# A recorded kernel with its own list scheduler, and the second MLP started from one finished chunk

## The chip, the cores and the metric

The kernel runs on one core of a Trainium2 chip. The metric is the device time of one execution in microseconds; three runs of the kernel before gave 1299.58 to 1303.39 us, with a median of 1301.85 us. The engines are named as in the profile: PE (TensorE; PEld its weight loads), DVE (VectorE), ACT (ScalarE), POOL (GpSimd) and SP (SyncE, which issues all DMAs here).

## The reference

Top-k attention over 4 batches, 8 heads, 576 positions of 64, followed by two MLPs on 2304 tokens of width 512 with an inner width of 2048. All is float32.

```python
def _attn_ref(q, k, v):
    top_k = 32
    scores = scale * np.matmul(q, k.transpose(0, 1, 3, 2))
    kth = np.partition(scores, -top_k, axis=-1)[..., -top_k:-top_k + 1]
    scores = np.where(scores >= kth, scores, -1000000000.0)
    scores = scores - np.max(scores, axis=-1, keepdims=True)
    attn = np.exp(scores)
    attn = attn / (np.sum(attn, axis=-1, keepdims=True) + 1e-09)
    return np.matmul(attn, v)

x = attn_out.transpose(0, 2, 1, 3).reshape(B * S, H * D)
h = x @ w_in1;  x = softplus(h) @ w_out1
h = x @ w_in2;  x = (h - np.tanh(h)) @ w_out2
```

## The kernel before

**Precision.** Every float32 operand of a matmul is split into two float16 halves, `hi` and `lo`, and a product is three matmuls (hi hi, hi lo, lo hi). So the weights of both MLPs must first be converted: 4 matrices of 8 groups each (`whi0` to `whi3`, `wlo0` to `wlo3`). `weight_load` brings one group of 1 MB, `weight_convert` and `weight_split` work on it with four ACT passes, two DVE passes and three POOL passes; `conv_step` does the one for a new group and the other for the one before it. Groups that find no free place in memory are staged in four pieces of 256 columns.

**Attention.** There are 144 tiles of 128 query rows by 576 keys. For a tile, `front` makes the scores (`s`, PE; copied to `ssb` by ACT), `chain` finds the 32 largest with four MAX8 and three MATCH_REPLACE8 on DVE, each of which needs the one before it, and `exps` makes the exponentials on ACT. Where the exponential table is loaded, that takes two ACT passes; where the softplus table is loaded, `exps` uses softplus, and `mask` adds a masking pass on DVE (L600) and a scaling pass on ACT (L601). `turn` splits the result (`hl`, ACT and POOL), transposes it by DMA (`pT`), and `back` multiplies it with the values (`px`, PE: 14 matmuls of 65 columns, or 28 of a rest tile) and writes the tokens (`xs`, then `x` by a transposing DMA).

**MLPs.** The tokens form 8 chunks of 256 and 2 rest chunks of 128; they become complete after attention tiles 16, 36, 52, 72 (two), 88, 108, 128 (two) and 144. For each chunk and MLP there are 8 steps, one for each pair of weight groups. A step is `gemm1` (`h`, 24 matmuls), `act1` (softplus or tanh on ACT, then ACT, POOL and, in the second MLP, one DVE pass) and `gemm2` (`y`, 24 matmuls of 256 columns or 12 of 512). The first MLP needs the softplus table, the second the exponential table; `set_table` changes it.

**What sets the order.** The program is written tile by tile in a loop over `n`. In each turn stand the attention pieces of up to four tiles, then `emit_steps` (one step of 256 tokens a turn, as long as `next_step` finds one), then `conv_step` by a credit: two groups a turn until 16 are done, then, from turn 8, half a group a turn. `next_step` allows the second MLP when all 32 groups are done and at least `MINC` = 2 chunks have begun; it prefers the second MLP when `AHEAD` = 2 chunks wait for it, then a new chunk's first MLP, then the second MLP of a waiting chunk. On each engine the framework's scheduler, which simulates the program, then orders the instructions; `tc.high_priority(n)` moves a block ahead by n places: 50 for attention, 1000 for the matmuls of `back`, 100 for the first 16 weight groups. The order on each engine is then fixed, and each engine takes its instructions one after the other. PSUM has two banks for `s`, four shared by `h`, `px` and the small column sums `pn`, and two for `y`.

Of the kernel before, what the change touches and what calls it, by code (L numbers as in the profile page):

```python
# [38 lines left out]
MINC = 2  # L39
# [6 lines left out]
W2N = 8  # L46
# [23 lines left out]
HP = 50  # L70
HPB = 1000
# [3 lines left out]
def topk_attention_two_mlps(  # L75
# [17 lines left out]
    nc = tc.nc  # L93
# [14 lines left out]
    cp = ctx.enter_context(tc.tile_pool(name="cp", bufs=1))  # L108
    dp = ctx.enter_context(tc.tile_pool(name="dp", bufs=1, space=bass.MemoryType.DRAM))
    wp = ctx.enter_context(tc.tile_pool(name="wp", bufs=1))  # L110
    ap = ctx.enter_context(tc.tile_pool(name="ap", bufs=1))
    sp = ctx.enter_context(tc.tile_pool(name="sp", bufs=2))
    mp = ctx.enter_context(tc.tile_pool(name="mp", bufs=1))
    ps_s = ctx.enter_context(tc.tile_pool(name="ps_s", bufs=1, space=bass.MemoryType.PSUM))
    ps_t = ctx.enter_context(tc.tile_pool(name="ps_t", bufs=4, space=bass.MemoryType.PSUM))
    ps_y = ctx.enter_context(tc.tile_pool(name="ps_y", bufs=1, space=bass.MemoryType.PSUM))

    first = tc.keep_in_program_order(nc.scalar.preload_act_table_set(EXP_SET))  # L120
    table = [first, [], EXP_SET]

    def set_table(name):
        if table[2] == name:
            return
        with ExitStack() as es_:
            for i in table[1] or [table[0]]:
                es_.enter_context(tc.issue_after(i.ins))
            table[0] = nc.scalar.preload_act_table_set(name)
        table[1], table[2] = [], name  # L130

    def with_table(out, in_, func, **kw):

        with tc.issue_after(table[0].ins):
            table[1].append(nc.scalar.activation(out, in_, func, **kw))  # L135

    zq = cp.tile([P, 2, 2, 2, D], F16, name="zq")
# [3 lines left out]
    tiles_ = cp.tile([P, 224], F32, name="tiny")  # L143
# [22 lines left out]
    def col_norm(cols, n):  # L166

        ps = ps_t.tile([P, 512], F32, tag="tp", name=nm("pn"))
        for i in range(n):
            nc.tensor.matmul(ps[:, 0:1], ones.to_broadcast([P, P]), cols[:, i : i + 1],  # L170
                             start=(i == 0), stop=(i == n - 1))
        return ps[:, 0:1]

    def pow2_scale(ps, s, inv):

        n = sp.tile([P, 1], I32, tag="n0", name=nm("n0"))
# [948 lines left out]
```

## Time and profile before

| | |
|---|---|
| median of three runs | 1301.85 us |
| span of the profiled execution (its time from first to last instruction) | 1304.4 us |
| PE busy | 1007.8 us (77%) |
| DVE busy | 1020.7 us (78%) |
| ACT busy | 959.4 us (74%) |
| POOL busy | 844.0 us (65%) |

The page gives the profiled execution by its span; it is 2.5 us above the median. The busy shares are means over stages that differ: attention begins at once, the first MLP at some 230 us, and in the last 186 us there is nothing but MLP work. So the time has to be read by stage. A row of the view by stage reads: from and to, length, then busy us and the number of instructions of PE, PEld, DVE, ACT and POOL, the mean granted TensorE clock (1.00 is 2.4 GHz), the DMA engines' share and GB/s. A matmul's row in a timeline shows its latency; as matmuls are pipelined, its cost is the time to the next start.

### The profile page before, as it was taken

The numbers are of one execution on the slowest core, as the hardware profiler recorded it, in microseconds if no ns is written. First come the engines' busy times: TensorE is split into PE (matmuls) and PEld (weight loads), VectorE is DVE, ScalarE is ACT, GpSimd is POOL, SyncE is SP. The second block draws the span as 40 slices with busy tenths as digits, with TensorE's granted clock in tenths as the row PEclk, the third lists the DMA queues.
The fourth block names the chain that finished last, engine by engine and source line by source line (L and its number), as shares of the span: only waits on it lengthen the run. The fifth ranks groups of instructions, "written<-read, shape, count | busy, mean of one in ns | idle before, by whom it ended". The sixth has DMA issues, their size and how long they took to land.

```text
span 1304.4 us, 27426 instructions
## 1 busy us (share of the span) xinstructions
PE 1007.8 (77%) x9682; PEld 793.1 (61%) x9682; DVE 1020.7 (78%) x2183; ACT 959.4 (74%) x1924; POOL 844.0 (65%) x1194
## 2 busy tenths in 40 slices
PE   1221324884436999899799899998999899999998
PEld 1111213763325877668667787786768767986975
DVE  5897889999999998899698879988989799510020
ACT  7987989878878878876787678877777677733332
POOL 2789767787687667566587657667776476643332
PEclk9999999896557999999799989998999899999999
DMA  9955887456666757745456444444545344200000
GB/s 276 281 162 146 240 233 170 122 119 138 140 145 159 169 102 146 147 86 125 84 128 137 75 89 90 105 101 89 127 104 119 60 85 97 51 6 13 5 9 17
DMA packets 322522, 153.14 MB, mean 117 GB/s; under 512 B 270160, under 2 KB 302416, under 8 KB 322384
## 3 DMA queue, kind: packets, MB, share of 16 engines
q1 hardware_dynamic: 322384, 151.39, 51.1%
q8 instruction: 76, 1.25, 0.4%
q14 instruction: 62, 0.51, 0.1%
HBM read 73.04 MB, written 15.37 MB: 68 GB/s over the span
## 4 chain that ended last, share of the span: by engine, by line
PE 29%; DVE 22%; ACT 13%; DMA 13%; POOL 12%; issue 8%; SPq 2%; POOLq 0%; ACTq 0%; DVEq 0%
DVE m L576 7%; DVE x L579 7%; PE h L692 4%; PE h L691 4%; PE h L693 4%; DMA pT<-hl 2%; POOL hl L607 2%; PE y L735 2%; DMA qT<-qhl 2%; PE y L736 2%; PE y L734 2%; PE y L742 2%; PE y L743 2%; PE y L744 2%; POOL wlo L317 2%
## 5 line engine op out<-in xcount | busy, mean ns | idle before, releaser
L576 DVE MAX8 m<-x 128x8 f32<-128x576 f32 x432 | 320.2, 750 | 3.9
L607 POOL TENSOR_TENSOR hl<-x,hl 128x512 f16<-128x512 f32 x144 | 170.1, 1182 | 87.5 <-ACT hl L606 84.5
L713 POOL TENSOR_SCALAR r<-r,gs 128x512 f32<-128x512 f32 (+1 forms) x160 | 112.5, 704 | 160.9 <-ACT g L712 158.8
L579 DVE MATCH_REPLACE8 x<-m,x 128x576 f32<-128x576 f32 x288 | 213.4, 741 | 0.0
L564 PE MATMUL s<-kT,qT 128*128 128x288 f16 x512 | 120.2, 326 | 98.2 <-ACT ssb L567 69.9
L716 POOL TENSOR_TENSOR g<-r,g 128x512 f16<-128x512 f32 (+1 forms) x160 | 171.7, 1074 | 8.6
L734 PE MATMUL y<-g,whi 128*128 128x256 f16 (+1 forms) x640 | 163.1, 266 | 10.5 <-DVE y L763 6.9
L691 PE MATMUL h<-x,whi 128*128 128x256 f16 (+1 forms) x640 | 168.2, 271 | 3.6 <-ACT x L647 1.6
L692 PE MATMUL h<-x,whi 128*128 128x256 f16 (+1 forms) x640 | 168.0, 270 | 0.0
L693 PE MATMUL h<-x,wlo 128*128 128x256 f16 (+1 forms) x640 | 167.7, 270 | 0.0
L735 PE MATMUL y<-g,whi 128*128 128x256 f16 (+1 forms) x640 | 164.5, 267 | 1.4 <-POOL g L716 1.4
L691 PE MATMUL h<-y,whi 128*128 128x256 f16 (+1 forms) x640 | 164.6, 265 | 0.1
L736 PE MATMUL y<-g,wlo 128*128 128x256 f16 (+1 forms) x640 | 164.3, 267 | 0.0
L692 PE MATMUL h<-y,whi 128*128 128x256 f16 (+1 forms) x640 | 164.2, 265 | 0.0
L693 PE MATMUL h<-y,wlo 128*128 128x256 f16 (+1 forms) x640 | 163.9, 264 | 0.0
L710 DVE SCALAR_TENSOR_TENSOR r<-h,hin,r 128x512 f32<-128x512 f32 (+1 forms) x80 | 54.9, 689 | 134.0 <-ACT r L135 133.5
L135 ACT ACTIVATE r<-h,hin 128x512 f32<-128x512 f32 (+1 forms) x160 | 102.1, 640 | 70.0 <-PE h L693 56.8
L712 ACT ACTIVATE g<-r,gs 128x512 f16<-128x512 f32 (+1 forms) x160 | 107.6, 675 | 52.7 <-DVE r L710 21.0
L692 PEld LDWEIGHTS <-whi 128*128 128x128 f16 x1280 | 128.3, 100 | 23.4 <-issue 7.6
L691 PEld LDWEIGHTS <-whi 128*128 128x128 f16 x1280 | 128.4, 100 | 20.6 <-DMA x<-xs 0.6
L693 PEld LDWEIGHTS <-wlo 128*128 128x128 f16 x1280 | 128.6, 101 | 13.7
L135 ACT ACTIVATE x<-ssb,nb,tiny 128x576 f32<-128x576 f32 x144 | 123.7, 865 | 15.3 <-DVE m L576 10.8
(141 smaller groups left out, 3058.9 us busy)
## 6 DMA issues: line engine op xcount, KB each, us to landing
whi<-in_moe_w_in_dram SPq DMA_DIRECT2D x8, 1024.0 KB, 5.9
wlo<-in_moe_w_in_dram SPq DMA_DIRECT2D x6, 1024.0 KB, 6.8
wlo<-in_moe_w_out_dram SPq DMA_DIRECT2D x6, 1024.0 KB, 5.0
vd<-vhl SPq DMA_DIRECT2D x16, 330.0 KB, 3.0
vhl<-vd SPq DMA_DIRECT2D x16, 330.0 KB, 3.4
kd<-kT SPq DMA_DIRECT2D x32, 160.0 KB, 2.1
whi<-in_moe_w_out_dram SPq DMA_DIRECT2D x5, 1024.0 KB, 5.0
kT<-kd SPq DMA_DIRECT2D x32, 160.0 KB, 2.6
```

Of the source, the lines that this page charges most:

```text
L135: table[1].append(nc.scalar.activation(out, in_, func, **kw))
L564: nc.tensor.matmul(ps[:, hf, 0:HS], lhs, rhs[:, hf * HS : (hf + 1) * HS], start=(i == 0), stop=(i == len(prods) - 1))
L576: return lambda: nc.vector.max(m[:, 8 * i : 8 * i + 8], src)
L579: return lambda: nc.vector.match_replace(x, m[:, 8 * i : 8 * i + 8], src, NEG)
L607: nc.gpsimd.tensor_sub(hl[:, S + SL : 2 * S], st.p[:, 0 : NB * P], hl[:, 0 : NB * P])
L691: nc.tensor.matmul(o, hi[:, f], xhi, start=(d == 0), stop=False)
L692: nc.tensor.matmul(o, hi[:, f], xlo, start=False, stop=False)
L693: nc.tensor.matmul(o, lo[:, f], xhi, start=False, stop=(d == ND - 1))
L716: nc.gpsimd.tensor_sub(glo, r, ghi)
L734: nc.tensor.matmul(o, hi[:, dd], gh, start=first, stop=False)
L735: nc.tensor.matmul(o, hi[:, dd], gl, start=False, stop=False)
L736: nc.tensor.matmul(o, lo[:, dd], gh, start=False, stop=fin)
```

## The change

It has four parts.

1. All calls go through a `Recorder`. It keeps each instruction with its reads and writes (so that the order of conflicting ones stays), a price by engine and size, and a rank: its place in the program, less what `ahead(n)` takes off. `order` then plays the program: at each point the engine that can start earliest takes, of the instructions whose inputs are there, the one of lowest rank; PE prefers those that have been ready for `MARG` = 500 ns. A `burst` of matmuls (a `px`, an `s`, half a `gemm1` or `gemm2`) stays together.
2. Weight groups 16 to 31 are converted at one a tile from turn 0 on (in effect from turn 8, since the first 16 come at two a tile until then), instead of half a one from turn 8.
3. The second MLP may begin when one chunk has begun its first (`MINC` = 1).
4. Attention has `ahead(200)`, the first 16 weight groups 100 as before. PSUM's four shared banks become two for `h` and two for `px` and `pn`. Tiles are laid out by hand (`al`), round robin over the same numbers of buffers.

```diff
-MINC = 2
+MINC = 1
-W2N = 8
+W2N = 0
-HP = 50
-HPB = 1000
+HP = 200
+HPB = 50
+NH = 2
+NPX = 2
+MARG = 500.0
...
+class Recorder:
...
+    def ahead(self, n):
+        was = self.off
+        self.off = max(n, was)
+        yield
+        self.off = was
...
+    def price(self, eng, method, a, k, outs, ins):
+        n = max(math.prod(x.shape[1:]) for x in outs + ins)
+        if eng == "PE":
+            cols = math.prod(out.shape[1:])
+            return (max(31.0, cols / 2.4 + 2.5) if ins[0].dtype == F16 else 250.0), 350.0
+        if eng == "SP":
+            if "transpose" in method:
+                return 1350.0, 2000.0
+            size = math.prod(out.shape) * mybir.dt.size(out.dtype)
+            return 480.0, 2000.0 + size / 300.0
+        if eng == "ACT":
+            if method == "copy":
+                return 70 + 0.82 * n, 160.0
+            c = 90 + 0.88 * n
+            c += 50 * sum(isinstance(k.get(x), View) for x in ("bias", "scale"))
+            return c + (95 if k.get("accum_out") is not None else 0), 160.0
+        if eng == "DVE":
+            if method == "max":
+                return 670.0, 140.0
+            if method == "match_replace":
+                return 735.0, 140.0
+            if n <= 8:
+                return 75.0, 140.0
+            return 60 + 1.22 * n, 140.0
+        if method == "memset":
+            return 100 + 0.4 * n, 100.0
+        if method == "tensor_scalar":
+            return 280 + 0.97 * n, 100.0
+        return 150 + 1.95 * n, 100.0
...
+            while coming[e] and coming[e][0][0] <= t:
+                r, i = heapq.heappop(coming[e])
+                heapq.heappush(avail[e], (ops[i].rank, i))
+            i = None
+            if margin.get(e):
+                aside = []
+                while avail[e]:
+                    x = heapq.heappop(avail[e])
+                    if ready[x[1]] <= t - margin[e]:
+                        i = x[1]
+                        break
+                    aside.append(x)
+                for x in aside:
+                    heapq.heappush(avail[e], x)
+            if i is None:
+                i = heapq.heappop(avail[e])[1]
...
-        ps = ps_t.tile([P, 512], F32, tag="tp", name=nm("px"))
+        ps = al("px", NPX, [P, 512], F32, pb)
-        with tc.high_priority(HPB):
+        with nc.ahead(HPB), nc.burst():
...
-        ps = ps_t.tile([P, 512], F32, tag="tp", name=nm("h"))
+        ps = al("h", NH, [P, 512], F32, pb)
...
-    WPS = 2
-    WPS2 = .5
+    WPS = WPSA
+    WPS2 = WPSB
...
+    nc.run(tc, {"PE": MARG})
```

`WPSA` is 2 and `WPSB` 1.0. In the new kernel every instruction is issued from one line (L334), so its rows tell apart by tile names; a number behind a name is the buffer. `pn` has no name of its own there (it is a `px`), nor have staged weights and the MLP inputs `x` and `y` (they are `xy`).

Three places in the order show what moved. The first is ACT where the table changes from softplus back to exponential for the first time. Before, 48 tiles' scores have been copied to `ssb` ahead of this load, and two chunks' first MLPs stand ahead of it; `r` and `g` are the MLP's activations, `xs` is attention's output, `qhl`, `khl` and `vhl` are split inputs:

```order
L542 ACTIVATE vhl_4925<-v_3911,tiny 128x10x64
L567 COPY ssb_4697<-s_4692 128x576
L647 ACTIVATE x_838_4410<-px_4670,r_889_4685 128x64
L655 CAST xs_4409<-x_838_4410 128x128
L135 ACTIVATE r_4619<-h_4594,hin_1809 128x512
L129 ACT_TABLE_LOAD
L135 ACTIVATE ssb_4420<-ssb_4420,m_4531 128x576
L513 CAST qhl_5560<-qraw_5071 128x512
L135 ACTIVATE ssb_4570<-ssb_4570,m_4658 128x576
L712 ACTIVATE g_4620<-r_4619,gs_1810 128x512
L135 ACTIVATE x_4532<-ssb_4420,nb_4779,tiny 128x576
```

Now, with 28 tiles copied and one chunk's first MLP done; `whi` from `xy` is a piece of a weight group:

```order
L334 ACTIVATE whi_0_71<-xy_0_99,tiny_64 128x256
L334 ACTIVATE whi_0_71<-xy_0_101,tiny_64 128x256
L334 ACTIVATE qraw_75<-qraw_75,tiny_64 128x256
L334 ACTIVATE x_2_136<-px_81,r_0_125 128x64
L334 CAST qhl_88<-qraw_75 128x512
L334 ACT_TABLE_LOAD
L334 ACTIVATE ssb_95<-ssb_95,m_106 128x576
L334 ACTIVATE ql_137<-ql_137,tiny_64 128x64
L334 CAST zq_63<-ql_137 64x128 x2
L334 ACTIVATE khl_83<-kraw_73,tiny_64 128x5x64
L334 ACTIVATE ssb_108<-ssb_108,m_115 128x576
```

The load, and with it the second MLP, stands 20 tiles earlier, among the last weight groups.

The second is DVE at the 88th tile's first MAX. Before (`x` is a tile's running copy of the scores, `m` its maxima):

```order
L576 MAX m_9267<-ssb_9155 128x8
L576 MAX m_9116<-x_9117 128x8
L579 MATCH_REPLACE x_9268<-m_9267,ssb_9155 128x576
L576 MAX m_9267<-x_9268 128x8
L600 SCALAR_TENSOR_TENSOR x_9117<-ssb_9034,m_9116,x_9117 128x576
L579 MATCH_REPLACE x_9268<-m_9267,x_9268 128x576
L576 MAX m_9267<-x_9268 128x8
L579 MATCH_REPLACE x_9268<-m_9267,x_9268 128x576
L576 MAX m_9267<-x_9268 128x8
L640 RECIPROCAL r_1640_9296<-r_1640_9296 128x1
```

Now:

```order
L334 MAX m_120<-ssb_92 128x8
L334 MAX m_115<-x_116 128x8
L334 MATCH_REPLACE x_94<-m_120,ssb_92 128x576
L334 MATCH_REPLACE x_116<-m_115,x_116 128x576
L334 MAX m_120<-x_94 128x8
L334 MAX m_115<-x_116 128x8
L334 MATCH_REPLACE x_94<-m_120,x_94 128x576
L334 SCALAR_TENSOR_TENSOR r_150<-h_149,hinb_164,r_150 128x512
L334 MAX m_93<-ssb_95 128x8
L334 RECIPROCAL r_0_125<-r_0_125 128x1
```

Before, a tile's MAX and MATCH_REPLACE often follow each other; now two tiles alternate, and no masking pass stands among them here.

The third is PE at the last tile's scores (`s`). Before:

```order
L564 LDWEIGHTS qT_15190
L564 MATMUL s_15712<-kT_15184,qT_15190 128x288
L692 LDWEIGHTS whi_89
L692 MATMUL h_15614<-x_12362,whi_89 128x256
L564 LDWEIGHTS qT_15190
L564 MATMUL s_15712<-kT_15184,qT_15190 128x288
L693 LDWEIGHTS wlo_90
L693 MATMUL h_15614<-x_12362,wlo_90 128x256
L691 LDWEIGHTS whi_89
L691 MATMUL h_15614<-x_12362,whi_89 128x256
```

Now:

```order
L334 LDWEIGHTS qT_113
L334 MATMUL s_91<-kT_86,qT_113 128x288
L334 LDWEIGHTS qT_113
L334 MATMUL s_91<-kT_86,qT_113 128x288
L334 LDWEIGHTS qT_113
L334 MATMUL s_91<-kT_86,qT_113 128x288
L334 LDWEIGHTS whi_0_65
L334 MATMUL h_153<-xy_0_100,whi_0_65 128x128
L334 LDWEIGHTS whi_0_65
L334 MATMUL h_153<-xy_0_100,whi_0_65 128x128
```

The scores are no longer interleaved with `h`, but one burst. Behind the last row of `s` stand 1702 matmuls of `h` and `y` before (886 of 256 columns, 240 of 512, 576 of 128) and 1452 now (768, 240, 444).

## Rows read from the trace of the kernel before

**Rows 1.** The page, busy us of each engine over the span (share, instructions).

```profile
PE 1007.8 (77%) x9682; PEld 793.1 (61%) x9682; DVE 1020.7 (78%) x2183; ACT 959.4 (74%) x1924; POOL 844.0 (65%) x1194
```

**Rows 2.** Busy us of each engine in seven stages (columns as told above).

```profile
0.00:196.00 196.00, 43.02 (x282) 30.39 (x282) 156.87 (x340) 167.73 (x303) 134.50 (x149) 1.00 0.80 223
196.00:300.00 104.00, 74.46 (x704) 60.56 (x705) 99.79 (x213) 89.29 (x178) 83.55 (x104) 0.95 0.61 131
300.00:392.00 92.00, 34.90 (x291) 26.61 (x291) 87.05 (x191) 74.26 (x183) 67.42 (x106) 0.54 0.61 146
392.00:457.00 65.00, 53.29 (x491) 44.86 (x491) 61.15 (x149) 54.42 (x124) 45.31 (x67) 0.84 0.70 167
457.00:784.00 327.00, 303.04 (x3028) 239.04 (x3028) 285.47 (x619) 249.89 (x510) 216.58 (x327) 0.96 0.56 111
784.00:1118.00 334.00, 317.92 (x3150) 249.21 (x3148) 301.36 (x620) 254.09 (x510) 224.34 (x345) 0.98 0.48 97
1118.00:1304.40 186.40, 181.19 (x1745) 142.42 (x1743) 28.96 (x59) 69.73 (x122) 72.26 (x101) 1.00 0.06 14
```

**Rows 3.** The same by stage, for the matmuls that write tile `h` alone.

```profile
300.00:392.00 92.00, 2.11 (x9) 0.54 0.61 146
```

**Rows 4.** PE's timeline, the last matmuls into `s` and the last of all.

```profile
L564 PE MATMUL s<-kT,qT x16: 283/286/286, 1093.1 to 1115.2; 128*128 128x288 f16 x16
...
1299.23 0.38 PE L744 MATMUL y<-whi,g 128*128 128x512 f16 x1
```

**Rows 5.** PE's timeline in the tail: start us, duration us, instruction.

```profile
1180.98 0.27 PE L691 MATMUL h<-y,whi 128*128 128x256 f16 x1
...
1183.60 0.38 PE L742 MATMUL y<-whi,g 128*128 128x512 f16 x1
1183.82 0.38 PE L743 MATMUL y<-wlo,g 128*128 128x512 f16 x1
```

**Rows 6.** Groups of like instructions: out<-in xcount | busy us, mean ns | idle before.

```profile
L600 DVE SCALAR_TENSOR_TENSOR x<-ssb,m,x 128x576 f32<-128x576 f32 x74 | 68.6, 931 | 7.5 <-ACT x L135 7.4
L288 DVE SCALAR_TENSOR_TENSOR whi<-whi 128x1024 int32<-128x1024 int32 (+1 forms) x18 | 21.8, 1216 | 18.8 <-ACT whi L282 18.7
L288 DVE SCALAR_TENSOR_TENSOR wst<-wst 128x256 int32<-128x256 int32 x18 | 13.3, 739 | 0.5 <-POOL r L713 0.5
L306 ACT ACTIVATE whi<-whi,tiny 128x1024 f16<-128x1024 f32 (+1 forms) x18 | 18.4, 1024 | 1.1 <-DVE tiny L180 1.1
L317 POOL TENSOR_TENSOR wlo<-wlo,whi 128x512 f16<-128x512 f32 (+1 forms) x29 | 33.8, 1181 | 0.5
L579 DVE MATCH_REPLACE8 x<-m,x 128x576 f32<-128x576 f32 x288 | 213.4, 741 | 0.0
L716 POOL TENSOR_TENSOR g<-r,g 128x512 f16<-128x512 f32 (+1 forms) x160 | 171.7, 1074 | 8.6
```

**Rows 7.** DVE's timeline: start us, duration us, instruction.

```profile
614.87 0.75 DVE L576 MAX8 m<-ssb 128x8 f32<-128x576 f32 x1
615.54 0.74 DVE L576 MAX8 m<-x 128x8 f32<-128x576 f32 x1
...
617.03 0.76 DVE L576 MAX8 m<-x 128x8 f32<-128x576 f32 x1
617.83 0.09 DVE L579 MATCH_VALUE_LOAD x<-m,x 128x8 f32 x1
```

**Rows 8.** The chain that ended last, in order of time: start, us, what.

```profile
1068.50 1.28 ACT L129
1069.80 0.88 ACT x L135
```

**Rows 9.** Whom DVE waited for from 196 to 1118 us: total, times, longest.

```profile
DVE m L576 <- ACT ssb L567: 20.7, 15, 7.0
DVE r L640 <- ACT r L639: 15.4, 14, 2.8
```

**Rows 10.** DVE's timeline, one row with the idle time before it.

```profile
628.13 0.76 DVE L576 MAX8 m<-ssb 128x8 f32<-128x576 f32 x1 [7.04 <-ACT ssb L567]
```

More of the change, by code (lines that the diff above doesn't have):

```diff
@@ new lines, with __init__, __getattr__ @@
+class Gen:
+    __slots__ = ("before", "users", "reads", "writes")
+    def __init__(self, before):
+        self.before, self.users, self.reads, self.writes = before, [], [], []
+class Op:
+    __slots__ = ("eng", "calls", "cost", "lat", "preds", "rank", "reads", "writes", "i", "start")
+class Queue:
+    def __init__(self, rec, eng, real):
+        self.rec, self.eng, self.real = rec, eng, real
+    def __getattr__(self, method):
+        return lambda *a, **k: self.rec.add(self.eng, getattr(self.real, method), method, a, k)
@@ L125, in set_table @@
             return
[L126 to L129, printed above, removed]
+        table[0] = nc.table(name, table[1] or [table[0]])
         table[1], table[2] = [], name
     def with_table(out, in_, func, **kw):
-        with tc.issue_after(table[0].ins):
-            table[1].append(nc.scalar.activation(out, in_, func, **kw))
-    zq = cp.tile([P, 2, 2, 2, D], F16, name="zq")
+        op = nc.scalar.activation(out, in_, func, **kw)
+        nc.after(op, table[0])
+        table[1].append(op)
+    zq = al("zq", 1, [P, 2, 2, 2, D], F16)
     nc.gpsimd.memset(zq, 0.0)
-    tiles_ = cp.tile([P, 224], F32, name="tiny")
+    tiles_ = al("tiny", 1, [P, 224], F32)
     used_ = [0]
@@ L166, in col_norm @@
     def col_norm(cols, n):
[L168 to L171, printed above, removed]
+        ps = al("px", NPX, [P, 512], F32, pb)
+        with nc.burst():
+            for i in range(n):
+                nc.tensor.matmul(ps[:, 0:1], ones.to_broadcast([P, P]), cols[:, i : i + 1],
+                                 start=(i == 0), stop=(i == n - 1))
         return ps[:, 0:1]
     def pow2_scale(ps, s, inv):
-        n = sp.tile([P, 1], I32, tag="n0", name=nm("n0"))
+        n = al("n0", 2, [P, 1], I32)
         nc.vector.tensor_scalar(n, ps.bitcast(I32), 24, 23,
@@ L778, in new_acc @@
     def new_acc(T):
-        return [ps_y.tile([P, 512], F32, tag="y", bufs=2, name=nm("y")) for _ in range(T // P)]
+        return [al("y", 2, [P, 512], F32, pb) for _ in range(T // P)]
     class Step:
@@ L842, in topk_attention_two_mlps @@
     for b in range(B):
-        groups = [[int(c) for c in w] for w in PLAN[b].split("_")]
+        groups = [[int(c) for c in w] for w in PLAN.split()[b].split("_")]
         for gi, ts in enumerate(groups):
```

378 lines of the change are left out of this document (278 added, 100 removed).

## The prediction

> **What bounds the kernel now.** I read the busy shares first, then busy time by stage, then the places where one engine starts or stops a kind of work, then the DVE's rows one by one.
>
> The shares alone say little: PE is busy 1007.8 us of 1304.4 [rows 1], with DVE close behind. The stages say more [rows 2]. After 1118 us PE is busy 181.2 of 186.4 us and DVE 29.0: attention is over and only MLP matmuls are left, back to back. From 457 to 1118 us PE is busy 621 of 661 us and DVE 587, so two engines share the limit. From 300 to 392 us DVE is busy 87 of 92 us, but PE only 34.9, at a granted clock of 0.54, which means nearly all of it at 1.2 instead of 2.4 GHz. And in those 92 us only 9 matmuls write an MLP hidden tile `h` [rows 3]: the first chunk's first MLP is done, the second MLP may not start because not all weights are converted (and because two chunks must have begun), and the next chunk's attention isn't finished. PE has a hole there and a queue of 184 us behind attention: the last score matmul starts at 1115.2 us and the last matmul of all at 1299.2 us [rows 4]. In that queue 24 matmuls of 256 columns start within 2.62 us, one in 0.109, and one of 512 columns holds PE for 0.22 [rows 5]: its full rate. So work moved from the queue into the hole is worth its PE time, provided that attention doesn't end later.
>
> The end is then: the time of the last score matmul (1115), plus the MLP matmuls that stand behind it on PE (184), plus the last store (5). I cost the change on these.
>
> **Term 1, the queue behind attention: 20 us less.** The order of instructions shows that the second MLP of chunk 0 now starts at attention tile 28 instead of 48 (there ACT first changes back to the exponential table). At tile 40 PE has put 197 thousand `h` and `y` columns behind it instead of 98. The lead shrinks later, because a chunk finishes only every 16 to 20 tiles and the steps run dry once at tile 71 to 75. Behind the last `s` row of PE's order there stand 1452 MLP matmuls instead of 1702: 118 fewer of 256 columns, 132 fewer of 128 columns, as many of 512. At 0.109 us for 256 columns [rows 5] and half of that for 128 (an estimate by the columns): 118 x 0.109 + 132 x 0.055 = 20 us. If small matmuls take as long as wide ones it is 27. Nothing hides this work, so the whole of it counts: -20.
>
> **Term 2, DVE's own work up to the last score: 20 us less, 18 taken.** DVE must do the whole top-k search. (a) While the softplus table is loaded, a tile's exponential needs a masking pass on DVE (74 of them, 0.93 us busy each [rows 6]). That table used to stay through the hole; now it is swapped out at tile 28, and the order holds 59 such passes. Neighbouring DVE rows overlap by about 0.1 us, so I take 0.8 us: 15 x 0.8 = 12 us less. (b) A MAX8 is followed 0.67 us later by an instruction of another tile, but 0.80 us later by one that needs its result [rows 7]; I take 0.12 us for each MAX8 or MATCH_REPLACE8. In the order of before 231 of them stand right behind the one they depend on, in the new order 140: 91 x 0.12 = 11 us less. (c) Conversions: two passes of 1024 fewer (1.2 us), eight of 256 more (0.7 us) [rows 6]: 3 us more. Sum -20. PE gets the same relief over the same stretch (from tile 40 to the last score 1197 thousand columns instead of 1248, 22 us), so it does not become the new limit by this. A little of it will fall into waits: -18.
>
> **Term 3, the early tiles: +4, from 0 to +15.** Between tiles 16 and 24 the new order has 19 conversion passes on DVE instead of 6, that is 9.5 weight groups instead of 3. A group costs DVE two 1024-wide passes, 2.4 us, and ACT (four passes of 1.0) and POOL (three of about 1.2) about 4 us each [rows 6], so those eight tiles hold 16 us more of DVE and 26 more of ACT. But by tile 16 one or two groups fewer are done, and from 24 to 48 one is left instead of six. At tile 48 the weights are done in both orders, and what is added by then on DVE is eight second-MLP passes (5 us), on ACT eight steps and table loads. DVE was the busy one there (87 of 92 us), ACT had 18 us free, POOL 25 [rows 2]. If all goes in parallel the cost is nothing, if the ACT work is exposed it is 15; nearest is DVE's row, +4.
>
> The table loads bear on this. The new order has 17 instead of 15, since the phases alternate at each chunk. The trace has 1.28 us for one, and the next activation starts 1.30 us after it [rows 8]: 2.6 us more on ACT, most of it beside DVE work. The Trainium skill (ScalarE: Activation LUTs, What ACT_TABLE_LOAD costs; Table sets: the hidden batching unit) speaks against this change: activations should be batched by table set, and a switch costs about 2.66 us, load and drain. By that it would be 5.3 us on ACT; the trace, with nothing behind the load, doesn't show the second half.
>
> **Term 4, waits: -18, from -60 to +60.** Up to 1118 us DVE is busy 992 us, the sum of six stages [rows 2], so 126 us of attention time are idle on DVE. Past 196 us the waits are of the kind that an order makes, not of one resource: on ACT's copy of the scores 20.7 us, on ACT's row sum 15.4 [rows 9], the longest 7.0 us before one MAX8 [rows 10]. The new order comes from a list scheduler with a price for each instruction. Its prices are near the rows: 735 ns for MATCH_REPLACE8 against 741, 1148 ns for a 512-wide POOL subtraction against 1074 [rows 6], 109 ns for a 256-column matmul against 109 [rows 5], 1283 ns for a table load against 1.28 us [rows 8]. What it doesn't price is the 0.12 us between dependent DVE instructions and the DMA engines' shared bandwidth. It always takes the oldest attention work first, and on PE prefers what has been ready for 500 ns, which guards against small errors. No row tells how well this comes out, so both ends stay: half of the idle time gone, or half as much again. I take one part in seven, because the prices fit and because the greedy rule feeds DVE first.
>
> **Sum:** 1304.4 - 20 - 18 + 4 - 18 = 1252. The span of the profiled execution lies 2.5 us above the median of the three runs (1301.85), so 1250 us.
>
> **Rivals.**
> 1. The waits stay and the DVE savings are half lost in them, because PE and DVE limit each other in turn (both around 90% from 457 us on [rows 2]). Then 1304.4 - 20 - 9 + 4 - 2.5 = 1277. For it: PE at 95% in the last stage of attention leaves little room. Against: PE gets 22 us less to do there. Chance 0.20.
> 2. The waits halve: 1304.4 - 20 - 20 - 60 - 2.5 = 1202. For it: the longest waits [rows 10] are those of a poor order. Chance 0.14.
> 3. The squeeze of weights at tiles 16 to 24 costs its 26 us of ACT in full and some 10 more in transfers that come too late, and nothing of it is recovered by tile 48: 1304.4 - 20 - 18 + 36 - 2.5 = 1300, no change. For it: DMA is busy 0.80 of the first 196 us [rows 2]. Chance 0.07.
> 4. Slower. The new order stands fixed on each engine, and one late instruction holds everything behind it there: a `px` burst of 14 matmuls that waits for its transposed tile now also holds the MLP matmuls behind it, an ACT pass that waits for a weight load holds the score copies that DVE needs. The 7.0 us before one MAX8 [rows 10] is the size of one such event. If DVE's idle time before the last score grows by half, 60 us, the time is 1304.4 - 20 - 18 + 10 + 60 - 2.5 = 1334. It decides from about 35 us of added waits, some five events of that size. Against: the order of before is fixed in the same way, with worse-fitting neighbours. The Trainium skill (TensorE: Matmul & The Clock Gate, Architectural detail) says that ACT and DVE take their queues strictly first in, first out; the trace agrees, in that DVE ran nothing in those 7.0 us. Chance 0.13.
> 5. The second MLP doesn't start early after all. The order excludes it (table load at tile 28), so its chance is within the others.
>
> **How the numbers follow.** The forecast, 1230 to 1270, gets 0.46. Differences under 0.3% (4 us) can't be told from no change here. Faster: forecast, rivals 1 and 2, 0.80. Within 0.3%: rival 3, 0.07. Slower: rival 4, 0.13. For 8 times in 10 the range takes in rival 1, rival 3 up to a little above it, and most of rival 2: 1205 to 1310.
>
> **What would show it.** Term 1: matmuls of the second MLP on PE between tiles 28 and 40, a granted clock well above 0.54 there, and 160 to 170 us between the last `s` matmul and the end. Term 2: 59 masking passes on DVE, and its busy time some 20 us below 1020.7. Term 3: tile 48 reached at 457 us or not much later. Term 4: DVE idle before the last score around 110 us instead of 126, last score at about 1080 us. Wrong it would be if that score came after 1115 us (then rivals 3 or 4: a late tile 48 says 3, new waits of PE on `pT` or of DVE on `ssb` later on say 4), or if PE idled behind it.

## The result: 2.4% faster, and the profile after

The new kernel takes 1272.2 us (median of four runs, 1270.15 to 1273.04). The kernel before took 1302.62 us beside it (1299.58 to 1304.87). The ratio is 0.9759, with an interval of 0.9733 to 0.9785. The forecast was 1250 and the range 1205 to 1310. The direction was right; the gain was 30 us where 52 were forecast.

The first part of the page of the new kernel (busy us, share of the span of 1269.9 us, instructions) answers to [rows 1]:

```profile
PE 997.0 (79%) x9688; PEld 783.6 (62%) x9688; DVE 1010.8 (80%) x2174; ACT 980.3 (77%) x1941; POOL 856.0 (67%) x1199
```

DVE lost 10 us of work, PE 11, and ACT gained 21. Most of the 34.5 us by which the span is shorter is therefore not work that went away. (The medians differ by 30.4 us. A run's time is 1.7 us above its span in the new kernel; by that the profiled execution of before was some 3 to 4 us slower than the median there.) The view by stage has columns as in [rows 2]. Its borders are the starts of attention tiles 16, 28, 40 and 48, the same 784 us as there (tile 96 starts at 786 us now and at 797 before), and the start of tile 143. The borders of [rows 2] lie near the same tiles, but for the first: tile 16 started at 210 us there.

```profile
0.00:207.00 207.00, 47.97 (x294) 34.00 (x295) 163.30 (x346) 170.06 (x291) 149.89 (x157) 1.00 0.76 214
207.00:348.00 141.00, 85.10 (x742) 69.62 (x741) 125.42 (x285) 127.64 (x299) 110.56 (x145) 0.94 0.55 129
348.00:421.00 73.00, 60.53 (x543) 42.27 (x543) 66.34 (x145) 63.66 (x137) 50.33 (x85) 0.92 0.72 145
421.00:471.00 50.00, 45.62 (x471) 39.30 (x469) 48.65 (x101) 45.02 (x92) 39.74 (x57) 0.99 0.82 176
471.00:784.00 313.00, 290.24 (x3018) 231.64 (x3017) 296.52 (x664) 260.90 (x525) 217.85 (x334) 0.97 0.58 118
784.00:1100.00 316.00, 303.81 (x3115) 241.22 (x3114) 282.82 (x582) 247.45 (x490) 221.71 (x332) 0.99 0.50 99
1100.00:1269.90 169.90, 163.68 (x1515) 125.52 (x1512) 27.71 (x59) 65.53 (x113) 65.91 (x91) 1.00 0.08 18
```

The hole of before is closed. Between tiles 28 and 40 PE is busy 60.5 of 73 us instead of 34.9 of 92, and its granted clock is 0.92 instead of 0.54. The same stage for the matmuls that write `h` alone (length, busy us and count, clock, DMA share, GB/s) has 200 of them, where [rows 3] has 9:

```profile
348.00:421.00 73.00, 25.50 (x200) 0.92 0.72 145
```

The price stands in the stage above it. Tile 28 starts at 347.6 us instead of 297.2, and of these 50 us 14 are left at tile 48 (471 instead of 457). From there on the new kernel wins. A row of the view by tile and a row of the timeline show the last scores and the last matmul, as in [rows 4]:

```profile
L334 PE MATMUL s<-kT,qT x28: 283/286/286, 1056.2 to 1098.7; 128*128 128x288 f16 x28
```

```profile
1265.29 0.38 PE L334 MATMUL y<-whi,g 128*128 128x512 f16 x1
```

The last score matmul starts at 1098.7 us (before 1115.2), and 171.2 us are left behind it (before 189.2).

### The profile page after: what moved, and what is told of

Same layout as the page of the kernel before. It is cut to its first block, busy times and chain, and to the rows that moved or that the text cites. A ratio compares the mean times of both kernels' runs of the same rounds, so it can differ in the third digit from the quotient of the medians.

```text
span 1269.9 us, 27324 instructions
## 1 busy us (share of the span) xinstructions
PE 997.0 (79%) x9688; PEld 783.6 (62%) x9688; DVE 1010.8 (80%) x2174; ACT 980.3 (77%) x1941; POOL 856.0 (67%) x1199
## 4 chain that ended last, share of the span: by engine, by line
PE 24%; DVE 9%; ACT 8%; POOL 7%; DMA 5%; issue 4%; SPq 1%; POOLq 0%; ACTq 0%; DVEq 0%
PE y L334 11%; PE h L334 10%; DVE x L334 4%; DVE m L334 4%; DMA pT<-hl 2%; POOL hl L334 2%; ACT x L334 2%; POOL g L334 2%; DMA qT<-qhl 2%; ACT r L334 1%; PE px L334 1%; POOL r L334 1%; PE s L334 1%; ACT ssb L334 1%; ACT hl L334 1%
## 5 line engine op out<-in xcount | busy, mean ns | idle before, releaser
L334 PE MATMUL h<-xy,whi 128*128 128x256 f16 (+1 forms) x2560 | 407.6, 267 | 9.2 <-ACT r L334 5.7
L334 PEld LDWEIGHTS <-whi 128*128 128x128 f16 x3840 | 361.9, 99 | 70.2 <-issue 10.1
L334 PE MATMUL h<-xy,wlo 128*128 128x256 f16 (+1 forms) x1280 | 329.9, 266 | 0.0
L334 DVE MAX8 m<-x 128x8 f32<-128x576 f32 x432 | 314.6, 747 | 2.6
L334 POOL TENSOR_TENSOR hl<-x,hl 128x512 f16<-128x512 f32 (+1 forms) x288 | 216.7, 769 | 86.2 <-ACT hl L334 76.8
L334 DVE MATCH_REPLACE8 x<-m,x 128x576 f32<-128x576 f32 x288 | 213.4, 741 | 0.0
L334 PE MATMUL y<-g,whi 128*128 128x256 f16 (+1 forms) x1280 | 202.0, 265 | 6.8 <-POOL g L334 4.9
L334 PEld LDWEIGHTS <-wlo 128*128 128x128 f16 x1920 | 190.7, 99 | 25.9 <-issue 5.4
L334 PE MATMUL y<-whi,g 128*128 128x512 f16 x576 | 193.1, 379 | 0.8 <-DVE xy L334 0.6
L334 POOL TENSOR_TENSOR g<-r,g 128x512 f16<-128x512 f32 (+1 forms) x160 | 174.7, 1092 | 21.8 <-PE y L334 7.6
L334 PE MATMUL y<-g,wlo 128*128 128x256 f16 (+1 forms) x640 | 164.0, 265 | 0.0
L334 PE MATMUL s<-kT,qT 128*128 128x288 f16 x512 | 96.8, 318 | 79.4 <-ACT ssb L334 64.1
L334 DVE SCALAR_TENSOR_TENSOR r<-h,hinb,r 128x512 f32<-128x512 f32 (+1 forms) x80 | 55.2, 692 | 129.6 <-ACT r L334 128.9
L334 PE MATMUL px<-vhl,pT 128*128 128x65 f16 (+1 forms) x2240 | 100.9, 201 | 54.6 <-DMA pT<-hl 23.0
L334 PEld LDWEIGHTS <-pT 128*128 128x128 f16 (+1 forms) x2240 | 93.2, 105 | 76.1 <-DMA pT<-hl 38.2
L334 ACT ACTIVATE x<-ssb,nb,tiny 128x576 f32<-128x576 f32 x144 | 124.3, 865 | 19.9 <-POOL nb L334 13.7
L334 PEld LDWEIGHTS <-g 128*128 128x128 f16 x864 | 82.8, 98 | 75.4 <-issue 1.2
L334 DVE MAX8 m<-ssb 128x8 f32<-128x576 f32 x144 | 108.0, 750 | 21.2 <-ACT ssb L334 21.0
L334 PEld LDWEIGHTS <-qT 128*128 128x128 f16 x512 | 53.2, 109 | 100.9 <-issue 59.4
L334 PE MATMUL y<-wlo,g 128*128 128x512 f16 x288 | 109.1, 379 | 0.0
L334 DVE MATCH_REPLACE8 x<-m,ssb 128x576 f32<-128x576 f32 x144 | 106.7, 741 | 0.3 <-issue 0.3
L334 ACT CAST hl<-x 128x576 f16<-128x576 f32 x144 | 96.5, 670 | 4.1 <-DMA pT<-hl 0.7
```

The lines of the kernel that those rows point to most:

```text
L334: fn(*a, **k)
```

## Experiments

Twelve kernels ran. Each row is read from that kernel's own trace. T24 and T48 are the starts of the first MAX8 of tiles 24 and 48, "last s" the start of the last score matmul, "behind" the rest of the span. Times and ratios (to before, with interval) are those of the timed runs. Before took 1302.1 us beside e1 to e4, 1304.5 beside e5 to e8 and 1301.6 beside e9 to e12.

| kernel | T24 | T48 | last s | behind | us | ratio |
|---|---|---|---|---|---|---|
| before | 265 | 457 | 1115 | 189 | 1302.6 | 1 |
| after | 313 | 471 | 1099 | 171 | 1272.2 | 0.976 (0.973 to 0.979) |
| e1: after, without the early steps | 262 | 451 | 1091 | 198 | 1291.9 | 0.993 (0.990 to 0.995) |
| e2: before, with the early steps | 290 | 495 | 1147 | 170 | 1318.4 | 1.012 (1.009 to 1.014) |
| e3: after, second MLP from two chunks | 310 | 469 | 1107 | 197 | 1306.4 | 1.003 (1.002 to 1.004) |
| e4: after, old pace of weights | 261 | 459 | 1096 | 187 | 1285.1 | 0.987 (0.985 to 0.989) |
| e5: after, three quarters of a group | 278 | 467 | 1089 | 172 | 1264.6 | 0.971 (0.967 to 0.974) |
| e6: after, SP prefers what is ready | 307 | 467 | 1092 | 172 | 1268.0 | 0.973 (0.970 to 0.975) |
| e7: after, attention not first | 315 | 471 | 1127 | 165 | 1294.2 | 0.993 (0.990 to 0.995) |
| e8: after, dependent DVE work priced | 313 | 471 | 1094 | 169 | 1264.6 | 0.969 (0.966 to 0.973) |
| e9: before, attention first | 259 | 456 | 1113 | 196 | 1314.4 | 1.011 (1.007 to 1.015) |
| e10: before, with all but the scheduler | 274 | 489 | 1138 | 171 | 1312.3 | 1.008 (1.005 to 1.011) |
| e11: e5, e6, e8 and e12 together | 277 | 468 | 1092 | 169 | 1261.1 | 0.969 (0.966 to 0.971) |
| e12: after, first tiles' preparation first | 306 | 464 | 1095 | 171 | 1264.0 | 0.971 (0.968 to 0.974) |

The constants are those of the diff: `MINC` and `W2N` with `WPSB` (`WPS2` before) are the two early steps, `HP` is how far attention goes first.

### Which part brings the gain: e1 and e2

e1 keeps the recorder and the list scheduler and takes the early steps out; e2 puts the early steps into the kernel before.

```diff
# e1, from after
-MINC = 1
+MINC = 2
-W2N = 0
+W2N = 8
-WPSB = 1.0
+WPSB = 0.5
# e2, from before
-MINC = 2
+MINC = 1
-W2N = 8
+W2N = 0
-    WPS2 = .5
+    WPS2 = 1.0
```

> The changed kernel with the old pace of weights (half a group a turn from turn 8) and MINC = 2: the recorder, its list scheduler and attention first, alone. Theory A (the gain has two sources, the shorter queue behind attention and fewer waits in the middle; early on the squeeze of weights costs some 14 us): no squeeze, no shorter queue (436 thousand columns behind the last scores instead of 423, +5 us), 74 masking passes as before, fewer waits between tiles 48 and 143 (some 20 us): about 1285 us, last scores at about 1095 us. Rival B (the list scheduler itself brings nothing, all comes from the earlier second MLP): 1302 us or more. Rival C (it brings all): 1272 us.

> The kernel before with only the numbers changed: MINC = 1, weights at one a turn from the first, framework's scheduler and old priorities. Theory A: queue behind attention 375 thousand columns instead of 423 (-20 us), 59 masking passes (-12), squeeze of weights (+14), waits as before: about 1285 us. Rival B: 1272 us. Rival C: 1300 us or more, and the last scores 20 us later than before.

e1 took 1291.9 us and e2 1318.4. The scheduler with its recorder, tile layout and ranks is worth 10 us alone (nearest to the 1285 of the theory that both parts gain), the early steps cost 16 us alone, and together they save 30. The parts don't add up. e2 came out where rival C had put it (1300 us or more, the last scores 20 us later; they came 32 later). The early steps did in e2 what term 1 says (170 us behind the last score instead of 189), but tile 48 came 38 us later. The largest loss is at tiles 24 to 28, four tiles in 65 us where before took 32. By stage, e2 reads there:

```profile
290.00:355.00 65.00, 50.76 (x507) 43.34 (x505) 44.57 (x108) 51.17 (x130) 49.50 (x78) 0.92 0.38 86
```

No engine is full there: DVE works 44.6 of 65 us, and ACT and POOL some 50.

### The two early steps need each other: e3 and e4

```diff
# e3, from after
-MINC = 1
+MINC = 2
# e4, from after
-W2N = 0
+W2N = 8
-WPSB = 1.0
+WPSB = 0.5
```

> The changed kernel with MINC = 2 alone: weights squeezed early, but the second MLP starts only with the second chunk, so nothing fills the hole. Theory A: the queue behind attention is the long one (436 thousand columns) and the squeeze is paid without use: slower than the scheduler alone by 5 to 14 us, about 1295 us. If the squeeze costs nothing in the end: the same as the scheduler alone.

> The changed kernel with the old pace of weights alone (MINC = 1): no squeeze, but weights are done only at tile 40, so the second MLP of the first chunk starts there, not at 28. Queue behind attention 418 thousand columns, 75 masking passes. Theory A: about 1282 us, last scores near 1095 us. If the squeeze is what holds the changed kernel back most (rival D): 1270 us or less.

With e1 and after this makes a square under the new scheduler:

| | two chunks must have begun | one chunk |
|---|---|---|
| half a weight group a tile | 1291.9 (e1) | 1285.1 (e4) |
| one group a tile | 1306.4 (e3) | 1272.2 (after) |

e4 came within 3 us of its theory (1285 us for 1282, the last score at 1096 for 1095). e3 did not: 1306 for about 1295. Faster weights alone cost 14 us: they delay tile 48 by 18 (469 instead of 451) and nothing uses them, so 197 us still stand behind the last score. The earlier second MLP alone gains 7 us, because it waits for the weights. With the weights there, it gains 34: e3 and after differ in `MINC` alone and start tile 48 within 2 us of each other, and everything gained comes behind it. The cost of the squeeze can be read from e4 and after (tile 48 at 459 or 471, 12 us) or from e1 and e3 (18 us).

### How dear the squeeze must be: e5, e6 and e12

e5 converts three quarters of a group a tile. e6 and e12 go at two waits of the new order. In the new kernel SP, which issues the transposes `pT` of attention, stood before one weight load. Its own timeline (start, us, what it issued) and its waits in 262 to 300 us (in total, times, longest):

```profile
272.70 4.05 SPq L334 DMA_TRANSPOSE pT<-hl  x2
276.85 0.52 SPq L334 DMA_DIRECT2D kT<-kd  x1
297.90 0.33 SPq L334 DMA_DIRECT2D whi<-in_moe_w_out_dram  x1
299.30 0.33 SPq L334 DMA_DIRECT2D wlo<-in_moe_w_out_dram  x1
299.82 1.62 SPq L334 DMA_TRANSPOSE pT<-hl  x1
```

```profile
SPq L334 <- DVE whi L334: 12.5, 1, 12.5
SPq L334 <- POOL wlo L334: 10.5, 4, 7.9
```

For 20.5 us (277.4 to 297.9) no transpose left, since the load waited for a place in memory that DVE and POOL still used. e6 gives SP the rule that PE has: prefer what has been ready for 2 us. e12 gives the preparation of the first tiles attention's rank, because the new kernel's first MAX8 starts at 41 us instead of 28.

```diff
# e5, from after
-WPSB = 1.0
+WPSB = 0.75
# e6, from after
-    nc.run(tc, {"PE": MARG})
+    nc.run(tc, {"PE": MARG, "SP": 2000.0})
# e12, from after
-    for i in range(LA - 1):
-        prep_for(tiles[i])
+    with nc.ahead(HP):
+        for i in range(LA - 1):
+            prep_for(tiles[i])
```

> The changed kernel with weight groups 16 to 31 at three quarters of a group a turn instead of one. The order of the MLP steps stays: table change at tile 29 instead of 28, the same 376 thousand columns behind the last scores, 61 masking passes. Squeeze theory (too many conversions between tiles 16 and 24 cost idle time of DVE that is not won back): tile 24 about 20 us earlier, tile 48 some 8 us earlier, the end about 1264 us. Rival (whatever is saved early is lost in the middle, since PE and DVE limit each other there): 1270 to 1274 us.

> The changed kernel with SP preferring DMAs that have been ready for 2 us by the scheduler's own clock. In the changed kernel SP stands still from 277 to 298 us before one weight load, with attention's transposes behind it. Queue theory (this wait is what the squeeze costs): the gap goes or shrinks, tile 24 comes 10 us earlier or more, the end some 8 us earlier, 1264 us. Rival (DVE and ACT convert weights in that gap anyway, so it costs little): 1272 us within 4.

> The changed kernel with only the first two tiles' preparation ahead of the first weight conversions. The first MAX8 came at 41 us instead of 28 because ACT converts weights ahead of the first keys. If time lost at the start is lost for good: 10 us less, 1262 us. If DVE wins it back by work that it must do anyway: 1270 to 1274 us.

All three were faster than after, by 4 to 8 us (of e6 the interval overlaps that of after, of e5 by a hair). e5 took the time that the theory of the squeeze gave, 1264.6 us, with tile 24 at 278 instead of 313 and as many columns done by the end of attention. But tile 48 came only 4 us earlier instead of 8; the other 6 were gained between tile 48 and the last score, of which the theory says nothing. In e6 the same stretch of SP's timeline is shorter, but not gone:

```profile
270.66 4.05 SPq L334 DMA_TRANSPOSE pT<-hl  x2
280.52 0.33 SPq L334 DMA_DIRECT2D kT<-kd  x1
291.92 1.27 SPq L334 DMA_TRANSPOSE pT<-hl  x1
```

Tile 24 comes 5 us earlier and tile 48 only 4, and the time lies between the two expectations. Even these are not the stand's: e6's rule also moved the first MAX8 from 41 to 32 us and tile 16 from 207 to 200, and from tile 16 to 24 e6 took 107 us, the new kernel 106. The stand cost nothing that shows; DVE was busy for 18.2 of its 20.5 us. In e12 the first MAX8 starts at 27 us; of the 14 us gained there, 7 are left at tile 48.

### Does DVE set the pace after tile 48? e7, e8 and e9

e7 lets attention go ahead by 50 only. e8 tells the scheduler that a DVE instruction behind the one it depends on costs 0.12 us more [rows 7]. e9 puts `HP` = 200 into the kernel before.

```diff
# e7, from after
-HP = 200
+HP = 50
# e8, from after
-                op.preds[j] = 0.0 if o.eng == op.eng and o.eng != "SP" else o.lat
+                op.preds[j] = (120.0 if op.eng == "DVE" else 0.0) if o.eng == op.eng and o.eng != "SP" else o.lat
# e9, from before
-HP = 50
+HP = 200
```

> The changed kernel with attention moved ahead by 50 places instead of 200, so that weight conversions (100) come first and MLP steps stand nearer. 263 dependent neighbours on DVE instead of 144 (0.12 us each, +14 us), 367 thousand columns behind the last scores instead of 376 (-4 us). If attention first matters: 1282 us or more. If it doesn't: 1268 us.

> The changed kernel whose scheduler knows 120 ns between two dependent DVE instructions. 83 dependent neighbours instead of 144: -7 us by the pitch that the trace of before shows (0.80 us against 0.67 after a MAX8). If DVE's own time sets the end of attention: 1265 us. If PE or the waits set it: 1272 us within 4.

> The kernel before with attention moved ahead by 200 places instead of 50, nothing else; the framework's scheduler. 94 dependent neighbours on DVE instead of 231, 439 thousand columns behind the last scores instead of 423 (+7 us). Theory (attention first is what makes the middle faster, whoever schedules): tiles 48 to 143 in about 635 us instead of 661, the end about 1285 to 1292 us, near the list scheduler alone (1291.9). Rival (it takes the list scheduler): 1300 us or more.

Attention first matters under the new scheduler: e7 reaches tile 48 at the same 471 us, and then its attention takes 31 us longer. Under the old one it costs 13 us (e9). For the question, the two stages up to and behind tile 48 are put side by side. First before, then after, e8, e9 and e7 (of e9 and e7 the second stage alone):

```profile
0.00:457.00 457.00, 205.67 (x1768) 162.42 (x1769) 404.86 (x889) 385.70 (x785) 330.78 (x423) 0.87 0.70 179
457.00:1118.00 661.00, 620.96 (x6174) 488.25 (x6174) 586.84 (x1238) 503.98 (x1019) 440.92 (x671) 0.97 0.52 104
```

```profile
0.00:471.00 471.00, 239.23 (x2047) 185.18 (x2048) 403.70 (x873) 406.38 (x816) 350.52 (x443) 0.97 0.70 174
471.00:1100.00 629.00, 594.05 (x6131) 472.86 (x6130) 579.35 (x1245) 508.35 (x1014) 439.56 (x666) 0.98 0.54 109
```

```profile
0.00:471.00 471.00, 238.55 (x2046) 185.21 (x2047) 389.20 (x868) 405.61 (x815) 348.38 (x443) 0.92 0.69 174
471.00:1096.00 625.00, 596.55 (x6173) 475.16 (x6172) 577.14 (x1254) 507.94 (x1020) 441.67 (x671) 0.98 0.55 109
```

```profile
456.00:1119.00 663.00, 611.33 (x6079) 479.34 (x6077) 572.22 (x1222) 495.87 (x1008) 436.97 (x665) 0.97 0.50 103
```

```profile
471.00:1132.00 661.00, 609.63 (x6237) 484.60 (x6236) 596.09 (x1249) 514.24 (x1026) 440.08 (x674) 0.96 0.51 104
```

e8 has 14.5 us less DVE work up to tile 48, and tile 48 comes at the same 471 us. e9 has 14.6 us less of it behind tile 48 (572.2 for 586.8), and the stage is 2 us longer. So what DVE saves was not passed on in these two kernels, one for each stage. (Both edits also change the order, so neither tests DVE's work alone.) e8's time of 1264.6 is the one expected if DVE set the pace, but it doesn't come from the place that this needs: some 5 us are gained between tiles 48 and 143 and some 3 behind, with 2 us less DVE work there; another order may do as much by itself. That PE sets the second stage fits better. I counted the matmuls that stand in each kernel's order behind the start of tile 48, at the pitches of the traces (0.109 us for 256 columns [rows 5], half of that for 128, 0.125 for an `s`, 0.034 for a `px` matmul):

| kernel | PE's need from tile 48 to the end | time it took | need / time |
|---|---|---|---|
| before | 784 | 847 | 0.926 |
| after | 745 | 799 | 0.933 |
| e1, e3, e4 | 782, 783, 780 | 838, 835, 824 | 0.933, 0.937, 0.947 |
| e5, e6, e8 | 745, 744, 745 | 794, 797, 791 | 0.939, 0.933, 0.941 |
| e11, e12 | 745, 745 | 792, 802 | 0.940, 0.929 |
| e7 | 742 | 821 | 0.904 |
| e2, e10 | 741, 742 | 822, 820 | 0.902, 0.904 |
| e9 | 781 | 853 | 0.915 |

The need is an estimate by count and pitch, but the pattern is plain. The need goes by 39 us as soon as the second MLP has both its steps. e3 and after, which differ in `MINC` alone, show it best: 38 us less need, 36 us less time. PE then runs at 93 to 95% of its need where list scheduler and attention first come together, and at 90% where one of them is missing and the steps are there; before, with none of the three, ran at 92.6%. At 745 us of need, 90 or 93% is a difference of 27 us.

### The rest without the scheduler, and the four edits together: e10 and e11

```diff
# e10, from before
-MINC = 2
+MINC = 1
-W2N = 8
+W2N = 0
-HP = 50
+HP = 200
-    WPS2 = .5
+    WPS2 = 1.0
```

e11 is after with the edits of e5, e6, e8 and e12.

> The same, with MINC = 1 and weights at one a turn as well: every part of the change but the recorder, its prices and its bursts. 381 thousand columns behind the last scores, 114 dependent neighbours, 59 masking passes. If the earlier second MLP only needs attention first to pay: 1275 us, near the changed kernel. If it needs the list scheduler (the squeeze of weights stalls attention in the framework's order, as between tiles 24 and 28 without attention first): 1300 us or more.

> The changed kernel with four small edits together: weights 16 to 31 at three quarters of a group a turn, 120 ns between dependent DVE instructions in the scheduler's model, SP preferring DMAs ready for 2 us, and the first two tiles' preparation ahead of the first weight conversions too. Each of the first three gave 4 to 8 us alone. If they add up and the start gains 10 us: 1245 us. If they take the same idle time: 1260 us.

e10 took 1312.3 us, 6 less than e2, so with the steps there the rank may help a little (the intervals of the two ratios overlap). But steps and rank don't pay without the recorder, that is, its order with its layout of tiles and its split of PSUM; which of these they need, no run says. e10's four tiles from 24 to 28 took 85 us (the new kernel's 35):

```profile
274.00:359.00 85.00, 58.62 (x576) 49.49 (x576) 52.80 (x127) 58.32 (x149) 51.97 (x82) 0.92 0.38 83
```

What ended most of DVE's idle time in that stretch of e10 (in total, times, longest):

```profile
DVE m L576 <- ACT ssb L567: 8.4, 3, 5.0
DVE x L579 <- POOL hl L608: 7.8, 4, 2.9
```

Other waits, of at most 3.7 us in total each, follow. These are small waits, for ACT, POOL and PE, of which the new kernel has less than 1 us from tile 24 to 28.

e11 took 1261.1 us, the lowest of all, and beats both kernels (its interval overlaps those of e5, e8 and e12). But e5, e8 and e12 alone were at 1264, and by the sum of the four gains it would have been 1245. By stage e11 reads

```profile
0.00:468.00 468.00, 239.36 (x2039) 185.28 (x2040) 398.87 (x874) 405.43 (x816) 347.52 (x443) 0.95 0.68 174
468.00:1094.00 626.00, 598.46 (x6184) 477.22 (x6182) 575.41 (x1250) 510.97 (x1020) 437.71 (x671) 0.98 0.54 110
```

Tile 48 still comes at 468 us, with ACT busy 405 of them, and PE still has its 94% behind it. So the gains of the four edits overlap; which slack they share, no run shows.

## Why the prediction was right in direction and too large

The 34.5 us of span fall into four pieces, as the forecast had them (DVE busy and idle are read from the view by stage with borders at the starts of tiles 48 and 143, 457.04 and 1117.93 us before, 471.0 and 1100.5 now, not at the last score; so the pieces add up to 35.4):

| piece | forecast | measured |
|---|---|---|
| term 1, behind the last score | -20 | -18.0 |
| term 2, DVE's own work | -18 | -8.1 |
| term 3, DVE idle up to tile 48 | +4 | +15.2 |
| term 4, DVE idle from tile 48 | -18 | -24.5 |
| profiled span to median | -2.5 | +2.3 |

So the 22 us by which the forecast was too low are in the main 10 of term 2 and 11 of term 3; term 4 gave back 7, and the profiled executions took 5.

**Term 1 was right**, in its mechanism and size, and its marks are there: 200 `h` matmuls in the hole, the clock of 0.92, 171 us behind the last score (160 to 170 were named). e3 and e4 show that this needs both steps (197 and 187 us behind).

**Term 2 was mis-sized.** Of the masking passes 59 are left, as forecast, and up to the last tile there are 13 fewer (72 before). But those that are left take longer. Groups of the new kernel (count, busy us and mean ns, then the idle time before them) answer to [rows 6]:

```profile
L334 DVE SCALAR_TENSOR_TENSOR x<-ssb,m,x 128x576 f32<-128x576 f32 x59 | 59.6, 1013 | 6.7 <-ACT x L334 6.5
L334 DVE SCALAR_TENSOR_TENSOR whi<-whi 128x1024 int32<-128x1024 int32 x26 | 38.6, 1485 | 6.0 <-ACT whi L334 5.9
L334 DVE SCALAR_TENSOR_TENSOR wlo<-wlo 128x1024 int32<-128x1024 int32 x22 | 35.1, 1596 | 4.9 <-ACT wlo L334 4.8
```

A masking pass went from 931 to 1013 ns. A conversion of 1024 columns did not become much dearer: the 1216 ns of [rows 6] are the mean of a line that holds passes of 1024 and of 256 columns. Before, by form, that line (L288) reads

```profile
L288 DVE SCALAR_TENSOR_TENSOR whi<-whi 128x1024 int32<-128x1024 int32 x13 | 19.4, 1491 | 18.8 <-ACT whi L282 18.7
L288 DVE SCALAR_TENSOR_TENSOR whi<-whi 128x256 int32<-128x256 int32 x5 | 2.4, 500 | 0.0
```

and all 50 passes of 1024 columns took 1484 ns in the mean, the 48 of now 1536. The forecast's 1.2 us was too low from the start. Up to the last tile, each instruction counted to the start of the next, (a) brought 5.9 us instead of 12 (61.6 to 55.7). Of (b) came 8.2 instead of 11 (MAX8, MATCH_REPLACE8 and their value loads, 719.3 to 711.1). (c) cost 5.2 us instead of 3 (103.0 to 108.2), and all other passes took 0.9 more. The price of a masking pass was taken from a trace in which it met fewer POOL instructions (last section).

That less DVE work brings the last score forward, as term 2 has it, is not shown either: e9 speaks against it behind tile 48 and e8 ahead of it. Rival 1 had this mechanism, that PE and DVE limit each other and DVE's savings are lost, and its time of 1277 is the nearest to the 1272 measured. But that is luck: it kept the waits as they were and the early tiles at +4, and neither came so.

**Term 3 was mis-sized, at the upper end of its bounds.** Tile 48 came 14 us later. I had taken the smaller end because DVE was the busy engine in [rows 2] and ACT had room. DVE's work up to tile 48 did stay the same (404.9 and 403.7 us), but its idle time there grew from 52.1 to 67.3 us. Tiles 16 to 24, before and now:

```profile
209.80:265.40 55.60, 38.05 (x337) 30.44 (x337) 53.34 (x119) 47.17 (x93) 43.59 (x58) 0.94 0.54 127
207.00:312.60 105.60, 58.88 (x494) 48.52 (x494) 91.47 (x210) 94.37 (x225) 79.92 (x100) 0.95 0.59 140
```

DVE has 38 us more work there instead of the 16 that I had counted, ACT 47 more instead of 26, and DVE stands idle for 14.1 us instead of 2.3. The number of conversions was right, their price was not: of the new kernel's passes there 8 are of 1024 columns and 44 of 256 (groups staged in pieces), and they take 39.7 us of DVE instead of 12.1. ACT was busy for 94 of the 106 us and ended 11 of the 14 us of waiting. The largest of these waits (207 to 313 us; in total, times, longest):

```profile
DVE xy L334 <- ACT xy L334: 3.6, 2, 2.2
DVE m L334 <- ACT ssb L334: 3.0, 2, 2.0
```

So the engine to price it from was ACT. The work comes back by tile 48; the idle time doesn't. Another 13 us of idle time stand ahead of the first tile, where ACT now converts weights first (17.6 to 26.3 us); 9 of them are won back by tile 16, and e12, whose first MAX8 starts at 27 us, reaches tile 48 7 us earlier. The squeeze itself costs 12 us from e4 to after and 18 from e1 to e3. The term had no place for the first tiles, which the ranks moved as well.

**Term 4 was right in sign and a little larger than taken**: DVE idle time behind tile 48 went from 74.2 to 49.7 us; up to the last tile's start 117 us are left, where 110 were named. The size was a guess. That the scheduler does it, e1 and e2 show: the same idle time is 58.4 us in e1, with the scheduler alone, and 74.2 in e2, with the steps alone. On [rows 9], for the stretch behind tile 48, first before (457 to 1118 us), then now (471 to 1100.5 us; `r` is both the row sum and the MLP's activation there, two rows before):

```profile
DVE m L576 <- ACT ssb L567: 20.1, 14, 7.0
DVE r L640 <- ACT r L639: 14.8, 12, 2.8
DVE r L710 <- ACT r L135: 11.2, 10, 4.3
```

```profile
DVE r L334 <- ACT r L334: 18.8, 27, 2.0
DVE m L334 <- ACT ssb L334: 12.6, 12, 5.3
```

The 7.04 us before one MAX8 [rows 10] have no like any more, the longest wait for `ssb` being 5.3. But it is not that waits of one kind went: those for `ssb` are down by 7.5 us, those for `r` by 7.2. The same stretch can be told from PE: 39 us less need behind tile 48, which at 93% are 42 us, some 6 more by the step from 0.926 to 0.933, and 14 lost ahead of tile 48. That gives 34, but it adds up by construction, since the share is need by time. What speaks for PE's account is that need and time fall together from e3 to after, while DVE's savings in e8 and e9 bought nothing in the stage where they were made.

**Rival 4 was wrong for this kernel, but its mechanism exists.** One late instruction did hold a queue, on SP, for 20.5 us, and shortening that in e6 made tiles 16 to 24 no faster. No kernel reached its sum of 1334; e2 (1318) and e10 (1312), the kernels with the steps and the old scheduler, came nearest. **Rival 3** had put the squeeze at 36 us by tile 48, where it was 14 in all.

**What stays open.** Why PE reaches 93% of its need under the list scheduler with attention first and 90% without, I can't reduce to one wait. Nor did a run part the recorder's own changes (PSUM in two pairs, the layout of tiles, prices, `MARG`) from each other; e1 has them all.

## What to carry to other kernels

When work is moved into a hole, count the need of the engine that sets the rest (here PE behind tile 48) before and after, and price what is put into the hole's run-up in the form in which it runs there (here pieces of 256 columns) and from the engine that has to do it there (here ACT), not from the one that looks busiest. A saving of 15 us on a second engine, 86 to 89% busy, bought nothing in its stage in two kernels here; take such a saving at little until a run shows otherwise. And parts of a change to an order don't add up: here the scheduler with the rank brought 10 us, the early steps alone cost 16 and the rank alone 13, and together they brought 30, so run the square with and without each.

## What the hardware showed that was not expected

A masking pass on DVE, which reads two tiles, takes 0.81 us in the median before and 0.82 now, and at most 1.8 us in both kernels. In e2 and e10 one of them took 6.71 and 7.93 us. The timelines of DVE and POOL in e10 (start, us, operation; the last line's bracket is the idle time before it):

```profile
308.19 7.93 DVE L600 SCALAR_TENSOR_TENSOR x<-ssb,m,x 128x576 f32<-128x576 f32 x1
```

```profile
307.87 1.86 POOL L313 TENSOR_SCALAR wst<-wst,tiny 128x256 f32<-128x256 f32 x4
309.70 1.14 POOL L716 TENSOR_TENSOR g<-r,g 128x512 f16<-128x512 f32 x1
310.83 0.68 POOL L713 TENSOR_SCALAR r<-r,gs 128x512 f32<-128x512 f32 x1
311.49 0.66 POOL L317 TENSOR_TENSOR wlo<-wst,whi 128x256 f16<-128x256 f32 x1
312.11 0.42 POOL L658 TENSOR_TENSOR xs<-x,xs 64x128 f16<-64x128 f32 x1
312.49 1.90 POOL L317 TENSOR_TENSOR wlo<-wst,whi 128x256 f16<-128x256 f32 x3
314.36 1.14 POOL L716 TENSOR_TENSOR g<-r,g 128x512 f16<-128x512 f32 x1
322.66 0.42 POOL L525 TENSOR_TENSOR zq<-ql,zq 64x128 f16<-64x128 f32 x1 [7.16 <-ACT zq L524]
```

POOL ran twelve instructions with no gap and went idle at 315.50 us. The DVE pass ended at 316.12, 0.62 us later. In e2 POOL's first gap came at 315.75 us and the DVE pass ended at 316.35, 0.60 us later. The two agree: the pass got through only when POOL paused. The Trainium skill (SBUF — State Buffer, Who interferes with whom) says that a DVE instruction with two inputs in SBUF contends with a POOL instruction that reads SBUF, over a port that is an exclusive lock. The trace agrees with the contention; but the longest of the twelve took 1.14 us, and the pass was held through all of them.

Short holds of this kind are common. In the new kernel 15 of the 59 masking passes took over 1.2 us; 14 of them began while a POOL instruction ran, and ended 0.61 to 0.62 us after its end. Before, it is 8 of 74, and all 8 did so. One of the new kernel's:

```profile
682.11 1.65 DVE L334 SCALAR_TENSOR_TENSOR x<-ssb,m,x 128x576 f32<-128x576 f32 x1 [0.29 <-ACT x L334]
681.99 1.16 POOL L334 TENSOR_TENSOR g<-r,g 128x512 f16<-128x512 f32 x1
```

POOL's instruction ended at 683.15 us and DVE's pass at 683.76. Over 0.82 us each, the 15 passes took 10.5 us in sum and the 8 of before 5.6. This 5 us is what lengthened the mean masking pass from 931 to 1013 ns. Why two passes were held through many POOL instructions and most long ones through one, no run shows.
